# Attention values in 64x64 quarters of the array, with the next scores between their two halves

## The chip, the cores and the metric

The kernel runs on one core of one Trainium2 chip. The metric is the device time of one launch in microseconds, as the median of several runs. One launch was also profiled, and every number taken from the profile belongs to that one execution.

## The reference

Eight batches of twelve attention heads, each with 448 tokens of 64 elements. Queries and keys are normalised by their root mean square, and the outputs of the heads, put side by side, are the rows of a feed-forward block.

```python
q_n, k_n = rmsnorm(q, g_q), rmsnorm(k, g_k)          # over the 64 elements
scores = q_n @ k_n.T / sqrt(64)
attn = softmax(scores)                               # over the keys
x = (attn @ v)                                       # (8, 12, 448, 64) -> (3584, 768)
h = x @ w_in                                         # (768, 1024)
solu = h * softmax(h)
ln = (solu - mean) / sqrt(var + 1e-6) * g_ln
out = ln @ w_out                                     # (1024, 768)
```

All of it is in fp32.

## The kernel before, in words

There are three stages: attention, the product with `w_in`, and the product with `w_out`. The second and third use a Strassen-like scheme of seven products (`products`, `outer_product`), with sums of blocks made by GpSimd. This text is about the first stage and its end.

**Quads.** Attention goes through 24 quads of four heads (`for m in range(NQ)`, NQ = 24). A quad is two pairs, `a = 2*m` and `b = 2*m + 1`; a pair holds two heads. The 448 keys of a head are three chunks of 128 (`kc` = 0, 1, 2) and a last chunk of 64. The code makes these units, in an order that is written out by hand and kept as it stands on every engine:

- `scores(n, kc)`: four matrix products of 64 rows by 64 columns of the array. Row half = head, column half = half of the 128 keys. They go into one two-bank PSUM tile (tag `t`, three of them). ScalarE (ACT) then makes the exponentials `E` (line 802).
- `scores_last(m)`: the same for the last 64 keys of both pairs (line 825).
- `values_last(m)`: the values of these last keys. Four 64x64 products open the accumulation of the output `o` of each pair (line 858).
- `values(n)`: the values of the three chunks, for one pair. Six products of 128 rows by 64 columns: all 128 keys of a chunk are contracted at once, and the two heads take the two column halves (line 869).
- `sums(m)`: the denominators of the softmax, by products with ones, 128 rows by 32 columns (line 891).
- `inverse(m)` and `divide(m)`: VectorE (DVE) inverts the sums, GpSimd (POOL) copies some of them across partitions (line 910), and VectorE spreads the inverses with a transpose (line 917) and multiplies `o` by them (line 918). `divide(m)` is put behind the first unit of the next quad.
- `store_x(m)`: the quad's result goes to DRAM, on the SP queue.

In a quad TensorE (PE) gets: scores a0, a1, a2, last, b0, b1, b2, `values_last`, values a, values b, sums. Beside it, ACT squares the queries and keys of two quads ahead (`squares`, line 672), multiplies those of the next quad by the gain (`gain`, line 727), computes reciprocal roots (lines 697, 698) and takes part in the conversion of `w_in` (lines 535, 536). DVE sums squares (line 680), transposes queries and keys (line 723) and adds exponentials (line 839). POOL folds the row sums (lines 690, 691), normalises (line 713) and adds exponentials (line 848).

**PSUM.** Six of the eight banks are the three `t` tiles. The other two have tag `o`: each pair's output takes one bank as a tile of its own. In the second stage the products `B` and `D` take them.

**The end of the stage.** After quad 22 (counted from 0) `load_x(0)` brings the first 256 rows of x back from DRAM, and `sizes(0)` squares them on ACT to check their size (line 951). It stands on ACT ahead of all exponentials of quad 23. In the quads 22 and 23 VectorE makes the additions of exponentials that POOL makes elsewhere (`on_vector`).

Of the kernel before, what the change touches and what calls it, by code (L numbers as in the profile page):

```python
# [9 lines left out]
FP32 = mybir.dt.float32  # L10
# [3 lines left out]
AF = mybir.ActivationFunctionType  # L14
OP = AluOpType
# [351 lines left out]
def fast_path(  # L367
# [24 lines left out]
    nc = tc.nc  # L392
    B, H, S, D = q.shape
    DM, DFF = moe_w_in.shape
    P = 128
    NJ = S // P
    NB = S // 32
    NP = H // 2
    NQ = B * NP // 2
# [4 lines left out]
    NG = NT // 2  # L404
# [11 lines left out]
    first, middle, banks_in = ExitStack(), ExitStack(), ExitStack()  # L416
# [201 lines left out]
    st = {}  # L618
    quads = {}
# [105 lines left out]
    def gain(n):  # L725
        d = st[n]
        nc.scalar.activation(d["qkT"][:, 0], d["qkT"][:, 0], AF.Copy, scale=gcol[:, KF : KF + 1])
# [32 lines left out]
    def warm_up():  # L760

        w = work.tile([P, 2, S], FP32, tag="r", name="warm", bufs=1)[:, 0]
        nc.vector.memset(w, 0.0)
        o = ps_t.tile([P, S], FP32, tag="o", name="pt", bufs=2)
        for _ in range(5):
            nc.tensor.matmul(o, w[:, 0:P], w, start=True, stop=True)

# [5 lines left out]

    def transpose_rows(n, s):
        d = st[n]
        d["pt", s] = ps_t.tile([P, S], FP32, tag="o", name="pt", bufs=2)
        for j in range(4):
            nc.tensor.transpose(d["pt", s][:, j * R : (j + 1) * R], d["qk"][:, s, j], ident[0:R, 0:R])

# [24 lines left out]
    def scores(n, kc):  # L804
        d = st[n]
        s = ps_t.tile([P, 2, 512], FP32, tag="t", name="s")

        for c in range(0, P, D):
            for h in range(2):
                hh = slice(h * D, (h + 1) * D)  # L810
                keys = slice(NJ * c + kc, NJ * (c + D - 1) + kc + 1, NJ)
                nc.tensor.matmul(  # L812
                    s[c : c + D, h, 0:S], d["qkT"][hh, 1, keys], d["qkT"][hh, 0, :],
                    start=True, stop=True,
                )
        exponentials(d, kc, s)
# [16 lines left out]
    def on_vector(m):  # L833
        return m >= NQ - 2

    def add(n):
        d = st[n]
        d["es"] = work.tile([P, 2, S], FP32, tag="es", name="es")
        nc.vector.tensor_tensor(d["es"], d["E", 0], d["E", 1], OP.add)  # L839

    def whole(n):
        return on_vector(n // 2) or n % 2 == 0

    def add_more(n):
        d = st[n]
        if whole(n):
            e = nc.vector if on_vector(n // 2) else nc.gpsimd
            e.tensor_tensor(d["es"], d["es"], d["E", 2], OP.add)  # L848

    def values_last(m):  # L850

        d = quads[m]
        for i in range(2):
            o = st[2 * m + i]["o"] = ps_t.tile([P, S], FP32, tag="o", name="o", bufs=2)
        for h in range(2):
            for i in range(2):
                pp = slice(i * D, (i + 1) * D)
                nc.tensor.matmul(  # L858
                    st[2 * m + i]["o"][h * D : (h + 1) * D, :], d["vl"][pp, h], d["E", NJ][pp, h],
                    start=True, stop=False,  # L860
                )

    def values(n):


        d = st[n]
        for kc in range(NJ):
            for h in range(2):
                nc.tensor.matmul(  # L869
                    d["o"][h * D : (h + 1) * D, :], quads[n // 2]["v"][:, n % 2 + 2 * h, kc], d["E", kc][:, h],  # L870
                    start=False, stop=(kc == NJ - 1),
                )
# [37 lines left out]
                nc.gpsimd.tensor_copy(rc[o : o + 32, :, t], rc[a : a + 32, :, t])  # L910

    def divide(m):
        xo = quads[m]["xo"] = work.tile([P, 2, S], FP32, tag="xo", name="xo", bufs=1)
        for i in range(2):
            n = 2 * m + i
            r = work.tile([P, NB, 32], FP32, tag="r", name="r", bufs=1)
            nc.vector.transpose(r, quads[m]["rc"][:, i].rearrange("p t b -> p (t b) ()").to_broadcast([P, NB, 32]))
            nc.vector.tensor_tensor(xo[:, i], st[n]["o"], r.rearrange("d b i -> d (b i)"), OP.mult)
            del st[n]

    def store_x(m):
        b, hp = divmod(2 * m, NP)
        xo = quads.pop(m)["xo"]
        rows = xd[b].rearrange("(g h i d) t -> h d g i t", h=2, i=2, d=D)
        for h in range(2):
            nc.sync.dma_start(rows[h][:, hp // 2], xo[h * D : (h + 1) * D])
# [5 lines left out]
    banks = []  # L932
# [12 lines left out]
    def sizes(g):  # L945

        x = gs[g, "x"].rearrange("p c t -> p (c t)")
        n = HD * 2 * P
        sm = gs[g, "s"] = xs.tile([P, 3, HD, P], FP32, tag="x", name="xsum")
        for i in range(2):  # L950
            nc.scalar.activation(
                sm.rearrange("p k c t -> p (k c t)")[:, 0:n], x[:, i * n : (i + 1) * n], AF.Square,
                accum_out=xmax[:, 2 * g + i : 2 * g + i + 1],
            )

# [20 lines left out]
    def products(g, done):  # L976


        k = {}
        n = DFF // 2  # L980

        def mul(bank, a, i, begin=True):
            a11, a12, a21, a22 = gs[g, "A"]
            sm = gs[g, "s"]
            a = {"a11": a11, "a12": a12, "s3": a21, "a22": a22, "s1": sm[:, 0], "s2": sm[:, 1], "s4": sm[:, 2]}[a]
            if begin:
                tag = "t" if bank in "AC" or bank == "B" and g == NG - 1 else "o"
                k[bank] = ps_t.tile([P, 512], FP32, tag=tag, name=bank, bufs=3 if tag == "t" else 2)[:, 0:n]
            for c in range(HD):
                nc.tensor.matmul(  # L990
                    k[bank], a[:, c], w_in[i][:, c],
                    start=begin and c == 0, stop=c == HD - 1, skip_group_check=not begin,
                )

        def part(name, bank):
            k[name] = sums_in.tile([P, 512], FP32, tag="part", name=name, bufs=4)[:, 0:n]
            nc.scalar.copy(k[name], k[bank])

        def plus(row, col, bank, x):
            t = 2 * g + row
            d = mt.setdefault(t, {})
            out = half_of(t, col)
            top = small.tile([P, 1], FP32, tag="top", name="top")
            nc.vector.tensor_tensor_reduce(
                out, k[bank], k[x], 1.0, d.get("top", -3.4e38), OP.add, OP.max, top
            )
            d["top"] = top

        def p1():
            mul("A", "a11", 0)
            part("q1", "A")

        def p2():
            mul("C", "a12", 1)
            plus(0, 0, "C", "q1")

        def p6():
            mul("A", "s2", 5, False)  # L1020
            part("u2", "A")

        def p5():
            mul("B", "s1", 3)

        def p7():
            mul("A", "s3", 4, False)
            part("u3", "A")
            plus(1, 1, "B", "u3")

        def p4():
            mul("D", "a22", 6)
            plus(1, 0, "D", "u3")
            done(1)

        def p3():
            mul("B", "s4", 2, False)
            plus(0, 1, "B", "u2")
            done(0)

        return {1: p1, 2: p2, 3: p3, 4: p4, 5: p5, 6: p6, 7: p7}
# [275 lines left out]
    def unit(f, steps=4):  # L1317
        nonlocal now
        f()
        now += steps  # L1320
        due = [x for x in todo if x[0] <= now]
        todo[:] = [x for x in todo if x[0] > now]
        for _, g in sorted(due, key=lambda x: x[0]):
            g()
# [26 lines left out]
    def step(m):  # L1351
        if m in sets:
            sets[m].pop(0)()
# [11 lines left out]
    with tc.manual_schedule():  # L1365
# [19 lines left out]
        for m in range(NQ):  # L1385
            a, b = 2 * m, 2 * m + 1

            def outputs():
                values_last(m)
                values(a)  # L1390


            next1 = m + 1 < NQ
# [52 lines left out]
                load_v(m + 1)  # L1446
            if m == 1:
                load(m + 3)
            unit(lambda: scores(a, 0))
            if m == 1:  # L1450
                gain(3)
            store_x(m - 1)
            if early:
                qk_transpose(a + 2)
                if next3 and m > 1:
                    load(m + 3)
            unit(lambda: scores(a, 1))
            unit(lambda: scores(a, 2))
            unit(lambda: scores_last(m))
            unit(lambda: scores(b, 0))  # L1460
# [4 lines left out]
            if not on_vector(m):  # L1465
                add_more(a)
            unit(lambda: scores(b, 2))
            if next2:
                squares(a + 4)
                squares(b + 4)  # L1470
                row_sums(a + 4)
            if next1:
                gain(a + 2)
                gain(b + 2)
            if next2:
                row_sums(b + 4)
                fold_sums(m + 2)
# [1 line left out]
            if on_vector(m):  # L1479
                add_more(a)  # L1480
                add_more(b)
            unit(outputs)
            step(m - 2)
            begin(m)
            step(m - 1)
# [4 lines left out]
                load_next()  # L1490
            if m == 3:
                norm_gain()
            unit(lambda: values(b))
            if m == NQ - 1:
                block_sums(0, 0)
                block_sums(0, 1)
# [4 lines left out]
                later(1, lambda m=m: divide(m))  # L1501
            if m == NQ - 2:
                load_x(0)
                sizes(0)
        divide(NQ - 1)
        store_x(NQ - 1)
        first.close()
# [185 lines left out]
```

## Time and profile before

| | |
|---|---|
| median of 3 runs | 802.65 us (802.65 to 802.79) |
| the profiled execution, its own time | 803.36 us |
| its span, first to last instruction | 801.6 us |
| TensorE clock granted | 0.999 |
| busy: PE, DVE, ACT, POOL | 98%, 77%, 59%, 65% |
| attention stage | from the start to about 316 us |
| one quad of it in the steady part | 12.51 us |

Busy time is the time in which at least one instruction of an engine is recorded as running. For PE it says little on speed, because up to four small products run side by side: a busy share of 98% may hide a rate that is lower than it could be. Each fp32 matrix product is recorded as two instructions, so a unit of four products appears as x8. The chain of waits goes back from the last instruction to what released it, and so shows which engine's time adds up to the span.

### The profile page before, as it was taken

The numbers are of one execution on the slowest core, as the hardware profiler recorded it, in microseconds if no ns is written. First come the engines' busy times: TensorE is split into PE (matmuls) and PEld (weight loads), VectorE is DVE, ScalarE is ACT, GpSimd is POOL, SyncE is SP. The second block draws the span as 40 slices with busy tenths as digits, with TensorE's granted clock in tenths as the row PEclk, the third lists the DMA queues.
The fourth block names the chain that finished last, engine by engine and source line by source line (L and its number), as shares of the span: only waits on it lengthen the run. The fifth ranks groups of instructions, "written<-read, shape, count | busy, mean of one in ns | idle before, by whom it ended". The sixth has DMA issues, their size and how long they took to land.

```text
span 801.6 us, 14271 instructions
## 1 busy us (share of the span) xinstructions
PE 788.1 (98%) x4854; PEld 462.7 (58%) x4854; DVE 613.7 (77%) x1202; ACT 472.2 (59%) x783; POOL 523.1 (65%) x664
## 2 busy tenths in 40 slices
PE   8999999999999999999999999999999999999997
PEld 4344444444444443444444444444789999999996
DVE  6787989989888896488878666777896776866945
ACT  6677878878778774376766544444515455464420
POOL 2666777778876784234456467668698777877861
PEclk9999999999999999999999999999999999999999
DMA  9878889897787832445554435552757457366312
GB/s 169 164 174 156 175 194 186 194 189 161 169 157 169 158 102 75 136 117 155 152 146 131 113 98 141 142 137 52 190 167 233 147 183 264 123 221 223 112 61 83
DMA packets 269598, 122.68 MB, mean 153 GB/s; under 512 B 187596, under 2 KB 254668, under 8 KB 269516
## 3 DMA queue, kind: packets, MB, share of 16 engines
q1 hardware_dynamic: 254332, 111.78, 55.9%
q10 hardware_dynamic: 15184, 9.90, 4.5%
q8 instruction: 40, 0.66, 0.3%
q14 instruction: 42, 0.34, 0.1%
HBM read 84.94 MB, written 36.70 MB: 152 GB/s over the span
## 4 chain that ended last, share of the span: by engine, by line
PE 87%; DVE 3%; DMA 2%; SPq 2%; POOL 2%; ACT 2%; issue 1%; DVEq 0%; ACTq 0%; POOLq 0%
PE A L1205 14%; PE A L990 13%; PE o L869 12%; PE s L812 12%; PE B L990 8%; PE B L1205 7%; PE C L990 4%; PE sm L891 4%; PE D L990 4%; PE C L1205 3%; PE s L825 2%; PE o L858 2%; SPq L636 1%; DMA xg<-xd 1%; ACT E L802 1%
## 5 line engine op out<-in xcount | busy, mean ns | idle before, releaser
L802 ACT ACTIVATE E<-s 128x896 f32<-128x896 f32 x168 | 138.8, 937 | 8.3 <-PE s L812 7.8
L812 PE MATMUL s<-qkT 64*64 64x448 f32 x1152 | 120.1, 545 | 1.0 <-ACT qkT L786 0.6
L869 PE MATMUL o<-E,v 128*64 128x448 f32 x576 | 113.8, 543 | 0.0
L1079 POOL TENSOR_TENSOR he<-he,mhalf 128x1 f32<-128x1 f32 x28 | 27.4, 977 | 102.5 <-DVE he L1078 97.4
L812 PEld LDWEIGHTS s<-qkT 64*64 64x64 f32 x1152 | 48.0, 163 | 59.4 <-ACT E L802 29.3
L1205 PE MATMUL A<-w_out,sums 128*128 128x192 f32 x392 | 79.9, 327 | 1.6 <-POOL sums L1185 1.2
L869 PEld LDWEIGHTS o<-E,v 128*64 128x64 f32 x576 | 39.1, 137 | 72.2 <-issue 68.0
L1205 PE MATMUL B<-w_out,sums 128*128 128x192 f32 x392 | 79.8, 326 | 0.5 <-DVE P L1267 0.5
L713 POOL TENSOR_TENSOR qkn<-qk,ny 128x896 f32<-128x896 f32 x46 | 77.2, 1699 | 3.8 <-DMA qk<-in_q_dram 1.5
L848 POOL TENSOR_TENSOR es<-es,E 128x896 f32<-128x896 f32 x22 | 46.4, 2110 | 48.8 <-ACT sq L672 34.0
L990 PE MATMUL B<-w_in,xsum 128*128 128x512 f32 x168 | 76.7, 592 | 0.0
L990 PE MATMUL A<-w_in,xg 128*128 128x512 f32 x168 | 74.6, 593 | 0.0
L1061 ACT ACTIVATE u<-h,hmax 128x1024 f32<-128x1024 f32 x28 | 32.2, 1148 | 66.8 <-DVE hmax L1055 66.8
L1205 PEld LDWEIGHTS A<-w_out,sums 128*128 128x128 f32 x392 | 66.1, 190 | 2.4 <-POOL sums L1185 1.5
L1205 PEld LDWEIGHTS B<-w_out,sums 128*128 128x128 f32 x392 | 66.2, 190 | 0.8 <-DVE P L1267 0.8
L839 DVE TENSOR_TENSOR es<-E 128x896 f32<-128x896 f32 x48 | 53.9, 1124 | 2.7 <-ACT E L802 2.7
L990 PEld LDWEIGHTS B<-w_in,xsum 128*128 128x128 f32 x168 | 31.9, 190 | 40.2 <-issue 39.2
L990 PEld LDWEIGHTS A<-w_in,xg 128*128 128x128 f32 x168 | 31.8, 190 | 40.1 <-issue 39.3
L690 POOL COPY ss<-part 32x56 f32<-32x56 f32 x92 | 47.0, 511 | 5.9 <-DVE part L680 1.4
L680 DVE TENSOR_REDUCE part<-sq 128x28 f32<-128x896 f32 x46 | 47.9, 1080 | 3.9 <-ACT sq L672 1.6
L723 DVE STREAM_TRANSPOSE qkT<-qkn 128x896 f32<-128x896 f32 x46 | 48.4, 1087 | 0.0
L563 POOL TENSOR_TENSOR w_out<-w_out 128x384 f32<-128x384 f32 x44 | 45.0, 1028 | 1.3
(153 smaller groups left out, 1651.0 us busy)
## 6 DMA issues: line engine op xcount, KB each, us to landing
ur<-ud SPq DMA_DIRECT2D x60, 256.0 KB, 4.6
ud<-ub SPq DMA_DIRECT2D x112, 128.0 KB, 2.3
xd<-xo SPq DMA_DIRECT2D x48, 224.0 KB, 3.0
qk<-in_q_dram SPq DMA_DIRECT2D x92, 112.0 KB, 3.1
qk<-in_k_dram SPq DMA_DIRECT2D x92, 112.0 KB, 3.0
v<-in_v_dram SPq DMA_DIRECT2D x24, 384.0 KB, 4.3
out_dram<-P SPq DMA_DIRECT2D x19, 384.0 KB, 4.2
raw<-in_moe_w_in_dram SPq DMA_DIRECT2D x12, 512.0 KB, 5.3
```

Source lines behind the costliest of these rows:

```text
L563: nc.gpsimd.tensor_tensor(o, p, q, OP.subtract)
L680: nc.vector.tensor_reduce(norms[m]["part"][:, i], st[n]["sq"], AX, OP.add)
L690: e.tensor_copy(ss[g * 32 : g * 32 + 32], part[o * 32 : o * 32 + 32])
L713: e.tensor_tensor(d["qkn"].rearrange("p (s b) d -> p s b d", s=2), d["qk"].rearrange("p s (b d) -> p s b d", d=32), y.rearrange("p (s b) - ...
L723: nc.vector.transpose(d["qkT"].rearrange("p s t -> p (s t)"), d["qkn"].rearrange("p b d -> p (b d)"))
L802: nc.scalar.activation(d["E", kc], s[:, :, 0:S], AF.Exp)
L812: nc.tensor.matmul(s[c : c + D, h, 0:S], d["qkT"][hh, 1, keys], d["qkT"][hh, 0, :], start=True, stop=True,)
L839: nc.vector.tensor_tensor(d["es"], d["E", 0], d["E", 1], OP.add)
L848: e.tensor_tensor(d["es"], d["es"], d["E", 2], OP.add)
L869: nc.tensor.matmul(d["o"][h * D : (h + 1) * D, :], quads[n // 2]["v"][:, n % 2 + 2 * h, kc], d["E", kc][:, h], start=False, stop=(kc == NJ ...
L990: nc.tensor.matmul(k[bank], a[:, c], w_in[i][:, c], start=begin and c == 0, stop=c == HD - 1, skip_group_check=not begin,)
L1205: nc.tensor.matmul(k[bank], a[:, c].rearrange("p a i -> p (a i)"), w_out[:, area, i, c], start=begin and c == 0, stop=c == KC - 1, skip_gr ...
```

## The change

**Quarters.** For the quads 1 to 22 (`halved(m)`) the values of both pairs are made by 64x64 products (`values_part`). A chunk's 128 keys are split in two halves of 64 rows. In part 0 pair a uses the keys in rows 0 to 63 and pair b those in rows 64 to 127, and in part 1 they exchange. So in each part a pair's bank is written from one row half only. Each part has 12 products instead of the 6 of `values(n)`.

**The first scores between.** Ahead of part 1 each row half must be done with the bank that the other row half is to write. `turn(m)` puts an empty instruction on ACT that waits for part 0's last product, and part 1's first product waits for it. Between the parts PE gets `scores(a + 2, 0)`, the first scores of the next quad, which are therefore missing at that quad's head. The quads 0 and 23 keep `values(a)`, `values(b)`.

**One tile.** Both pairs' outputs are one two-bank tile; `divide` makes one transpose and one product of 896 columns instead of two of 448 each. The tiles of the start (`pt`) and `B`, `D` of the second stage are paired likewise.

**Order on ACT.** `gain(a + 2)` goes ahead of the squares and `gain(b + 2)` behind the turn. `sizes(0)` goes behind the last exponentials of quad 23, and writes its squares into a work tile.

**One addition** of the last pair (47) goes from DVE to POOL.

The SP queue has the same instructions in the same order.

```diff
     def transpose_rows(n, s):
         d = st[n]
-        d["pt", s] = ps_t.tile([P, S], FP32, tag="o", name="pt", bufs=2)
+        if s == 0:
+            d["pt"] = ps_t.tile([P, 2, 512], FP32, tag="o", name="pt", bufs=1)
+        d["pt", s] = d["pt"][:, s, 0:S]
...
     def add_more(n):
         d = st[n]
         if whole(n):
-            e = nc.vector if on_vector(n // 2) else nc.gpsimd
+            e = nc.vector if on_vector(n // 2) and n < 2 * NQ - 1 else nc.gpsimd
...
     def values_last(m):
         d = quads[m]
+        o = d["o"] = ps_t.tile([P, 2, 512], FP32, tag="o", name="o", bufs=1)
         for i in range(2):
-            o = st[2 * m + i]["o"] = ps_t.tile([P, S], FP32, tag="o", name="o", bufs=2)
+            st[2 * m + i]["o"] = o[:, i, 0:S]
...
+    def values_part(m, part):
+        first = None
+        for kc in range(NJ):
+            for i in range(2):
+                d = st[2 * m + i]
+                pp = slice((part ^ i) * D, (part ^ i) * D + D)
+                for h in range(2):
+                    x = nc.tensor.matmul(
+                        d["o"][h * D : (h + 1) * D, :], quads[m]["v"][pp, i + 2 * h, kc], d["E", kc][pp, h],
+                        start=False, stop=(part == 1 and kc == NJ - 1),
+                    )
+                    first = first or x
+        if part == 0:
+            quads[m]["half"] = x
+        else:
+            behind(first, quads[m]["turn"])
...
+    def turn(m):
+        x = quads[m]["turn"] = nc.scalar.nop()
+        behind(x, quads[m]["half"])
...
     def divide(m):
-        for i in range(2):
-            r = work.tile([P, NB, 32], FP32, tag="r", name="r", bufs=1)
-            nc.vector.transpose(r, quads[m]["rc"][:, i].rearrange("p t b -> p (t b) ()").to_broadcast([P, NB, 32]))
-            nc.vector.tensor_tensor(xo[:, i], st[n]["o"], r.rearrange("d b i -> d (b i)"), OP.mult)
+        r = work.tile([P, 2 * NB, 32], FP32, tag="r", name="r", bufs=1)
+        nc.vector.transpose(r, d["rc"].rearrange("p i t b -> p (i t b) ()").to_broadcast([P, 2 * NB, 32]))
+        nc.vector.tensor_tensor(xo, d["o"][:, :, 0:S], r.rearrange("d (i b) x -> d i (b x)", i=2), OP.mult)
...
             def outputs():
                 values_last(m)
-                values(a)
+                if halved(m):
+                    values_part(m, 0)
+                else:
+                    values(a)
...
-            unit(lambda: scores(a, 0))
             if m == 1:
+                unit(lambda: scores(a, 0))
                 gain(3)
+            else:
+                unit(lambda: scores(a, 1))
...
             unit(lambda: scores(b, 2))
+            if not next1:
+                sizes(0)
+            if next1:
+                gain(a + 2)
             if next2:
                 squares(a + 4)
                 squares(b + 4)
                 row_sums(a + 4)
-            if next1:
-                gain(a + 2)
-                gain(b + 2)
...
             unit(outputs)
+            if halved(m):
+                turn(m)
+                gain(b + 2)
...
-            unit(lambda: values(b))
+            if halved(m):
+                unit(lambda: scores(a + 2, 0))
+                unit(lambda: values_part(m, 1))
+            else:
+                unit(lambda: values(b))
...
             if m == NQ - 2:
                 load_x(0)
-                sizes(0)
```

More of the change, by code (lines that the diff above doesn't have):

```diff
@@ L763, in warm_up @@
         nc.vector.memset(w, 0.0)
-        o = ps_t.tile([P, S], FP32, tag="o", name="pt", bufs=2)
+        o = ps_t.tile([P, 2, 512], FP32, tag="o", name="pt", bufs=1)[:, 0, 0:S]
         for _ in range(5):
@@ L839, in add, with halved @@
         nc.vector.tensor_tensor(d["es"], d["E", 0], d["E", 1], OP.add)
+    def halved(m):
+        return 0 < m < NQ - 1
     def whole(n):
@@ L861, in values_last, with behind @@
                 )
+    def values_part(m, part):
[14 more added lines that the diff above has]
+            behind(first, quads[m]["turn"])
+    def behind(x, y):
+        tc.add_manual_dep(
+            getattr(x, "ins", x), getattr(y, "ins", y).name,
+            mybir.DependencyInfo(mybir.DependencyClass.Sync, mybir.DependencyReason.DATA),
+            reason="row tiles change banks",
+        )
+    def turn(m):
+        x = quads[m]["turn"] = nc.scalar.nop()
+        behind(x, quads[m]["half"])
     def values(n):
@@ L912, in divide @@
     def divide(m):
-        xo = quads[m]["xo"] = work.tile([P, 2, S], FP32, tag="xo", name="xo", bufs=1)
-        for i in range(2):
-            n = 2 * m + i
-            r = work.tile([P, NB, 32], FP32, tag="r", name="r", bufs=1)
-            nc.vector.transpose(r, quads[m]["rc"][:, i].rearrange("p t b -> p (t b) ()").to_broadcast([P, NB, 32]))
-            nc.vector.tensor_tensor(xo[:, i], st[n]["o"], r.rearrange("d b i -> d (b i)"), OP.mult)
-            del st[n]
+        d = quads[m]
+        xo = d["xo"] = work.tile([P, 2, S], FP32, tag="xo", name="xo", bufs=1)
+        r = work.tile([P, 2 * NB, 32], FP32, tag="r", name="r", bufs=1)
+        nc.vector.transpose(r, d["rc"].rearrange("p i t b -> p (i t b) ()").to_broadcast([P, 2 * NB, 32]))
+        nc.vector.tensor_tensor(xo, d["o"][:, :, 0:S], r.rearrange("d (i b) x -> d i (b x)", i=2), OP.mult)
+        for i in range(2):
+            del st[2 * m + i]
     def store_x(m):
@@ L949, in sizes @@
         sm = gs[g, "s"] = xs.tile([P, 3, HD, P], FP32, tag="x", name="xsum")
+        y = sm.rearrange("p k c t -> p (k c t)")
+        if g == 0:
+            y = work.tile([P, 2 * NB, 32], FP32, tag="sq", name="sq", bufs=2).rearrange("p b d -> p (b d)")
         for i in range(2):
             nc.scalar.activation(
-                sm.rearrange("p k c t -> p (k c t)")[:, 0:n], x[:, i * n : (i + 1) * n], AF.Square,
+                y[:, 0:n], x[:, i * n : (i + 1) * n], AF.Square,
                 accum_out=xmax[:, 2 * g + i : 2 * g + i + 1],
@@ L986, in mul @@
             if begin:
-                tag = "t" if bank in "AC" or bank == "B" and g == NG - 1 else "o"
-                k[bank] = ps_t.tile([P, 512], FP32, tag=tag, name=bank, bufs=3 if tag == "t" else 2)[:, 0:n]
+                if bank in "AC" or bank == "B" and g == NG - 1:
+                    k[bank] = ps_t.tile([P, 512], FP32, tag="t", name=bank, bufs=3)[:, 0:n]
+                else:
+                    if "BD" not in k:
+                        k["BD"] = ps_t.tile([P, 2, 512], FP32, tag="o", name="BD", bufs=1)
+                    k[bank] = k["BD"][:, "BD".index(bank), 0:n]
             for c in range(HD):
@@ L1456, in fast_path @@
                     load(m + 3)
-            unit(lambda: scores(a, 1))
+            if m == 1:
+                unit(lambda: scores(a, 1))
             unit(lambda: scores(a, 2))
@@ L1492, in fast_path @@
                 norm_gain()
-            unit(lambda: values(b))
+            if halved(m):
+                unit(lambda: scores(a + 2, 0))
+                unit(lambda: values_part(m, 1))
+            else:
+                unit(lambda: values(b))
             if m == NQ - 1:
```

## The prediction

> **What bounds the kernel now.** I read the page first: busy times and the chain that ended last.
>
> ```profile
> PE 788.1 (98%) x4854; PEld 462.7 (58%) x4854; DVE 613.7 (77%) x1202; ACT 472.2 (59%) x783; POOL 523.1 (65%) x664
> ...
> PE 87%; DVE 3%; DMA 2%; SPq 2%; POOL 2%; ACT 2%; issue 1%; DVEq 0%; ACTq 0%; POOLq 0%
> ```
>
> PE is busy for 98% and holds 87% of the chain, so time comes only from what PE executes, from gaps in it, or from the rate at which small products run side by side. For the rate I read the chain over a steady stretch (start, duration, what).
>
> ```profile
> 205.31 0.75 PE s L825 x8
> 206.06 2.25 PE s L812 x24
> 208.32 0.75 PE o L858 x8
> 209.07 4.66 PE o L869 x24
> 213.73 1.65 PE sm L891 x32
> 215.38 2.45 PE s L812 x24
> ```
>
> The reader is to see that no engine but PE is in it, and the rates. 64x64 products: 0.75 us for 8 instructions, 2.25 for 24, so 0.094 each. 128x64 products: two beside each other instead of four, so 24 should take 24 x 0.188 = 4.51; the line has 4.66, which is 0.15 more. The trace's single records show where: 64x64 products start in groups of four every 0.376 us, values in groups of two every 0.376, but from the last group of line 858 to the first of line 869 it is 0.485, and to the next 0.427. That is 0.11 + 0.05 = 0.16 us for going from 64x64 to 128x64. The groups of sums (0.189 apart) and of scores show the same at their heads: 2.45 against 2.25 is 0.20, and 1.65 against 32 x 0.047 = 1.50 is 0.15. Quad 3 confirms it: a 128-row transpose between its two values costs each of them the entry (2.40 and 2.41 instead of 2.25). So a quad of 12.51 us pays three changes of shape, half a microsecond together.
>
> The gaps of PE are few: of those after the start, the longest but one is in quad 23. In order of time on PE, then ACT (start, duration; in brackets the idle time before and what ended it):
>
> ```profile
> 302.68 2.52 PE L812 MATMUL s<-qkT 64*64 64x448 f32 x24
> 306.21 0.98 PE L825 MATMUL s<-qkT 64*64 64x448 f32 x8 [1.01 <-ACT E L802]
> 307.02 2.62 PE L812 MATMUL s<-qkT 64*64 64x448 f32 x24
> 309.47 0.93 PE L858 MATMUL o<-E,vl 64*64 64x448 f32 x8
> ```
> ```profile
> 303.45 0.84 ACT L951 ACTIVATE xsum<-xg 128x768 f32<-128x768 f32 x1 [5.08 <-DMA xg<-xd]
> 305.26 5.74 ACT L802 ACTIVATE E<-s 128x896 f32<-128x896 f32 x7
> ```
>
> ACT waits 5.08 us for the DMA of x with the size check at its head; the seven exponentials stand behind it, all three `t` tiles fill up and PE stops. In other quads line 825 starts 2.34 us after the first scores, here 3.53; later pieces are 0.06 and 0.19 late. Together 1.44 us.
>
> **What the Trainium skill says.** TensorEngine Tiling (Array Packing), Key Properties: changing the tiling mode, not just the tile, drains TensorE. The trace agrees and prices it at 0.15 to 0.20 us. The same page, Gotcha 1: different row tiles can't use one PSUM bank at the same time; that is why the turn must exist. The trace has no case of it, but `values_last` already writes each bank from one row half, at the full 0.376 us per group of four. PSUM — Partial Sum Buffer, Engine vs sequencer instructions: a sequencer instruction waits for earlier ones to be dispatched, not to complete. The trace agrees: ACT's semaphore events for the squares stand at 220.91 to 221.15, while the exponential ahead of the last one was still running (to 221.36). No price of a page is used.
>
> **The change part by part.**
>
> *Quarters.* Removed: 12 products (24 instructions) of 128x64. Added: 24 products (48 instructions) of 64x64, at 0.094 each 4.51 us, the same as 24 x 0.188. The order of the quarters differs from that of the scores (row halves change every second product), but these four are also all different, and line 858 shows four quarters with four separate streams at full rate. What goes is the entry of 0.16 us, since everything from the first scores to part 1 is now 64x64. The entry to sums (0.15) stays, from 64x64 instead of 128x64: not seen before, so it may be anything from 0 (a gain of another 0.15 per quad) to 0.30 (the saving is lost there); I take 0.15, as all the entries seen lie at 0.15 to 0.20. The scores moved between the parts keep the shape, and the next quad's a1 pays the 0.20 that a0 paid. 22 quads x 0.16 = **3.5 us less**.
>
> *The turn.* Part 1's first product waits for ACT, which waits for part 0's last product. Behind it on PE are the rest of part 1, the sums and the next quad. With zero at the first scores after the sums, PE's new course is: a1 to b2 and `values_last` until 5.34, part 0 until 7.59, next a0 until 8.34, part 1 until 10.60. Part 0's last product ends at 7.77 (a record is 0.54 long). PE's end at 220.835 and ACT's next event at 220.908 give a hop of 0.07; two hops make 7.95, a weight load 0.14, so 8.1 against 8.34: 0.25 us to spare. ACT must have reached the turn by then. Its six exponentials start at 1.08 (after the reciprocal roots, as now), 0.80 apart, and end at 6.0; gain to 6.6; squares to 8.3. If ACT's sequencer is one instruction ahead, it is at the turn by 7.5. So I take 0. From both sides: no gain, since the wait only adds; at worst the turn falls behind the finished squares, 8.3 + 0.07 + 0.14 = 8.5, and 0.2 us per quad. Behind it on ACT stand `gain(b + 2)` (due 5 us later), the conversion and the next a0's exponential, whose tile is wanted again only by the next a2.
>
> *Scores ahead.* a0 of the next quad is wanted at 7.59, its gain done at 6.6, its queries transposed on DVE at about 5.2. E takes an eighth buffer of eight; the ninth is written only after part 1 has read the first. ACT's tightest point was b2, whose tile came free at 219.74 and which began at 219.90, 0.17 us later; six exponentials instead of seven leave 0.24. Nothing is late, 0.
>
> *One divide.* DVE saves two starts: 2 x (0.65 + 0.63) = 2.56 becomes about 2.1 (a transpose of 896 columns takes 1.09 on line 723). It lies beside PE, and brings the transposes forward until they meet POOL's normalise (ends at 220.68, the transpose of it began at 220.87), some 0.15. The quad gets shorter by about the same, so POOL's fold, which releases ACT's roots just in time (215.70, roots done at 216.36, scores ready at 216.31), stays where it was relative to PE. One tile for both banks must be read out before `values_last`, 3 us later: 0. In the second stage B's release is the last of its group either way: 0.
>
> *Size check.* The 1.44 us of quad 23 go: x lands at about 300 and ACT comes to it at about 305, after its exponentials. Its reader on POOL is wanted 5 us after the end of the sums. **1.4 us less.** The last addition on POOL takes 2.1 us where DVE took 1.0; it is wanted 2 us later by the sums, and the block sums behind it are still 5 us early: 0.
>
> Sum: 3.5 + 1.4 = 4.9. The profiled execution took 803.36 us (span 801.6, 1.8 around it), 0.7 above the median: 798.5, and from the median of 802.65, **797.7 us**.
>
> **Rivals.**
> 1. *Only the check counts.* The change of shape is not saved but paid at the sums or the parts (0.16 per quad). For: the sums change rows and columns at once. Against: each entry in the trace costs 0.15 to 0.20 whatever the pair of shapes. 802.65 - 1.4 = 801.2, no change.
> 2. *The turn holds PE* (slower). If ACT reaches the turn only once both squares have completed, and each hop takes 0.2 instead of 0.07, part 1 starts at 8.8 instead of 8.34: 0.45 per quad. 22 x (0.45 - 0.16) = 6.4, less 1.4: 807.6. It decides from a stall of 0.22 us per quad (0.16 + 1.4 / 22). For: the spare time is only 0.25 us. Against: the events of ACT run ahead of its engine.
> 3. *The sums' entry goes too*, in part: 22 x 0.1 less, 795.5.
>
> **How the numbers follow.** Main course 0.70, rival 1 or a small stall of the turn 0.13, rival 2 with its milder forms 0.10, rival 3 0.07. The measurement can tell about 0.2% (1.6 us) from no change. Faster: main, rival 3 and a part of rival 1, 0.81; same 0.09; slower 0.10. The range goes from rival 3, 795.5, to the worst that I worked out for the turn, 0.2 per quad: 22 x (0.2 - 0.16) = 0.9, less 1.4, 802.1. It takes in rival 1; the worse part of rival 2 and a full loss of the sums' entry stay out.
>
> **What would show it.** Right: between the sums no engine but PE in the chain, a quad of 12.35 us, line 858's successor at 2.25 per part, quad 23 without a gap before line 825's successor. Wrong: idle time before part 1 released by ACT's sequencer, parts slower than 2.25, or sums above 1.65.

## The result and the profile after

The changed kernel takes 802.2 us (median of 20 runs, 801.27 to 803.93); the kernel before took 803.43 us in the same comparison (20 runs, 802.49 to 804.52). The ratio is 0.9985, 95% interval 0.9979 to 0.9991: 1.2 us less, where the prediction had 4.9 less. The profiled execution has a span of 800.4 us instead of 801.6.

First the page of the changed kernel: busy times, and shares of the chain that ended last.

```profile
PE 786.5 (98%) x5382; PEld 468.7 (59%) x5382; DVE 609.0 (76%) x1153; ACT 473.1 (59%) x783; POOL 524.3 (66%) x665
...
PE 86%; DVE 5%; SPq 2%; issue 2%; ACT 1%; DMA 1%; POOL 1%; DVEq 0%; ACTq 0%; POOLq 0%
```

PE has lost 1.6 us of busy time and still holds the chain: the bound is the same. The chain of waits over a steady stretch (start, duration, what):

```profile
205.88 2.25 PE s L814 x24
208.14 0.75 PE o L864 x8
208.89 2.25 PE o L878 x24
211.15 0.75 PE s L814 x8
211.90 2.25 PE o L878 x24
214.15 1.65 PE sm L927 x32
215.80 1.70 PE s L814 x16
```

This is what the prediction asked for. Each part has 2.25 for 24 instructions, so two parts take 4.50 where the two values took 4.66; the next quad's scores lie between them; the sums still pay their entry (1.65); no other engine is in it. A steady quad, from the start of its sums to that of the next, is 12.37 us instead of 12.52 (given as 12.51 above).

Quad 23, on PE and then on ACT, in order of time:

```profile
302.17 1.77 PE L814 MATMUL s<-qkT 64*64 64x448 f32 x16
303.76 0.93 PE L827 MATMUL s<-qkT 64*64 64x448 f32 x8
304.51 2.44 PE L814 MATMUL s<-qkT 64*64 64x448 f32 x24
306.76 0.93 PE L864 MATMUL o<-E,vl 64*64 64x448 f32 x8
```
```profile
303.25 4.97 ACT L804 ACTIVATE E<-s 128x896 f32<-128x896 f32 x6 [3.80 <-PE s L814]
308.05 0.90 ACT L990 ACTIVATE sq<-xg 128x768 f32<-128x768 f32 x1
```

No gap is left on PE, and the check of `x` (line 990) stands behind the exponentials. So every step that the prediction named in the attention stage is there, and the time isn't. The table takes the span apart by the starts of PE's instructions. It also has a second profile of each kernel, taken later (experiments 10 and 11).

| us | before | before, 2nd | after | after, 2nd |
|---|---|---|---|---|
| start to the sums of quad 0 | 23.39 | 23.43 | **25.26** | **25.25** |
| to the sums of quad 1 | 14.72 | 14.69 | 15.26 | 15.24 |
| to the sums of quad 22 | 263.18 | 263.18 | 260.13 | 260.14 |
| to the sums of quad 23 | 13.71 | **12.97** | 11.64 | 11.62 |
| to the second stage | 1.27 | 1.27 | 1.27 | 1.27 |
| second stage, first to last product | 252.03 | 252.02 | **252.89** | **252.88** |
| third stage, first to last product | **227.23** | 227.90 | 227.80 | 227.82 |

The three rows between the sums of quad 0 and of quad 23 hold what was predicted: 291.6 - 287.0 = 4.6 us less (3.8 against the second profile of before). Two costs stand against it. The start is 1.85 us later, and the second stage is 0.86 longer. The start of the changed kernel on PE, and of the kernel before:

```profile
8.74 1.16 PE L780 MATMUL pt<-ident,x 112*128 112x112 f32 x8 [0.47 <-PE pg L491]
11.11 2.52 PE L814 MATMUL s<-qkT 64*64 64x448 f32 x24 [1.21 <-ACT qkT L788]
13.56 0.60 PE L780 MATMUL pt<-ident,x 112*128 112x112 f32 x4
15.30 0.60 PE L780 MATMUL pt<-ident,x 112*128 112x112 f32 x4 [1.14 <-ACT qkT L786]
```
```profile
10.58 2.52 PE L812 MATMUL s<-qkT 64*64 64x448 f32 x24 [0.62 <-ACT qkT L786]
13.03 0.98 PE L778 MATMUL pt<-ident,x 112*128 112x112 f32 x8
```

Two things are to be seen. The first scores begin at 11.11 instead of 10.58. And the second pair's eight transposes, one group at 13.03 before, are cut into four at 13.56 and four at 15.30, with a wait for ACT's line 786 between. ACT of the changed kernel shows the other side:

```profile
10.00 0.64 ACT L786 ACTIVATE qkT<-pt,gcol 128x448 f32<-128x448 f32 x1 [0.47 <-PE pt L780]
...
14.60 0.65 ACT L786 ACTIVATE qkT<-pt,gcol 128x448 f32<-128x448 f32 x1
```

The first copy out of `pt` needs only the first four transposes, but it waits for all eight. The later one stands behind three exponentials (from 12.19 on), and the next transposes, which write the other bank, wait for it. Both banks are one tile since the change; the explanation to be tested is that each wait here is for the whole tile (experiments 1 to 4).

The second stage shows the same, on PE and on DVE:

```profile
365.44 1.98 PE L1033 MATMUL BD<-w_in,xg 128*128 128x512 f32 x4
```
```profile
364.69 0.69 DVE L1049 CUSTOM_DVE_ANT_0 h<-BD,u 128x512 f32<-128x512 f32 x1 [2.02 <-ACT u L1040]
365.31 0.08 DVE L1049 DVE_READ_ACCUMULATOR2_ANT top<- 128x1 f32 x1
```

From the last `A` product's start to the first `BD` product's it is 0.28 us longer than the usual 0.43: that product, bank D's first, starts at 365.44, when DVE has finished reading bank B (its event stands at 365.40). The next start is 0.10 late as well, and the pair comes once more at 419.

### The profile page after: what moved, and what is told of

Read it like the earlier page. It is cut to its first block, busy times and chain, and to the rows that moved or that the text cites. A ratio compares the mean times of both kernels' runs of the same rounds, so it can differ in the third digit from the quotient of the medians.

```text
span 800.4 us, 15291 instructions
## 1 busy us (share of the span) xinstructions
PE 786.5 (98%) x5382; PEld 468.7 (59%) x5382; DVE 609.0 (76%) x1153; ACT 473.1 (59%) x783; POOL 524.3 (66%) x665
## 4 chain that ended last, share of the span: by engine, by line
PE 86%; DVE 5%; SPq 2%; issue 2%; ACT 1%; DMA 1%; POOL 1%; DVEq 0%; ACTq 0%; POOLq 0%
PE A L1248 14%; PE s L814 13%; PE o L878 12%; PE BD L1033 11%; PE A L1033 11%; PE B L1248 7%; PE sm L927 5%; PE C L1033 5%; PE C L1248 3%; PE s L827 2%; PE o L864 2%; SPq L636 1%; DVE ub L1137 1%; DVE bs L1116 1%; PE o L905 1%
## 5 line engine op out<-in xcount | busy, mean ns | idle before, releaser
L804 ACT ACTIVATE E<-s 128x896 f32<-128x896 f32 x168 | 141.4, 932 | 12.8 <-PE s L814 11.6
L814 PE MATMUL s<-qkT 64*64 64x448 f32 x1152 | 123.9, 544 | 1.6 <-ACT qkT L788 1.2
L878 PE MATMUL o<-E,v 64*64 64x448 f32 x1056 | 107.1, 536 | 0.0
L853 POOL TENSOR_TENSOR es<-es,E 128x896 f32<-128x896 f32 x23 | 49.1, 2137 | 51.4 <-DVE es L841 51.4
L878 PEld LDWEIGHTS o<-E,v 64*64 64x64 f32 x1056 | 40.2, 133 | 58.4 <-issue 58.4
L1033 PE MATMUL BD<-w_in,xsum 128*128 128x512 f32 x156 | 71.2, 592 | 0.0
L841 DVE TENSOR_TENSOR es<-E 128x896 f32<-128x896 f32 x48 | 57.1, 1193 | 0.7 <-ACT E L804 0.7
L723 DVE STREAM_TRANSPOSE qkT<-qkn 128x896 f32<-128x896 f32 x46 | 50.9, 1106 | 4.1 <-POOL qkn L713 4.1
L1033 PEld LDWEIGHTS BD<-w_in,xsum 128*128 128x128 f32 x156 | 29.5, 190 | 37.5 <-issue 35.1
L1248 PE MATMUL A<-w_out,s 128*128 128x192 f32 x224 | 45.6, 326 | 0.5 <-ACT u L1260 0.5
```

The lines of the kernel that those rows point to most:

```text
L723: nc.vector.transpose(d["qkT"].rearrange("p s t -> p (s t)"), d["qkn"].rearrange("p b d -> p (b d)"))
L804: nc.scalar.activation(d["E", kc], s[:, :, 0:S], AF.Exp)
L814: nc.tensor.matmul(s[c : c + D, h, 0:S], d["qkT"][hh, 1, keys], d["qkT"][hh, 0, :], start=True, stop=True,)
L878: x = nc.tensor.matmul(d["o"][h * D : (h + 1) * D, :], quads[m]["v"][pp, i + 2 * h, kc], d["E", kc][pp, h], start=False, stop=(part == 1 a ...
L1033: nc.tensor.matmul(k[bank], a[:, c], w_in[i][:, c], start=begin and c == 0, stop=c == HD - 1, skip_group_check=not begin,)
L1248: nc.tensor.matmul(k[bank], a[:, c].rearrange("p a i -> p (a i)"), w_out[:, area, i, c], start=begin and c == 0, stop=c == KC - 1, skip_gr ...
```

## Experiments

The lines of kernels 1, 2, 3, 8 and 9 stand some lines further down than those of the changed kernel, because of a helper at the top.

### 1. The start in tiles of its own

```diff
-        o = ps_t.tile([P, 2, 512], FP32, tag="o", name="pt", bufs=1)[:, 0, 0:S]
+        o = two[1].tile([P, S], FP32, tag="o", name="pt", bufs=2)
...
-        if s == 0:
-            d["pt"] = ps_t.tile([P, 2, 512], FP32, tag="o", name="pt", bufs=1)
-        d["pt", s] = d["pt"][:, s, 0:S]
+        d["pt", s] = two[1].tile([P, S], FP32, tag="o", name="pt", bufs=2)
```

`two` is a pool for these two banks alone, closed and opened again behind the start; the rest is the changed kernel.

> The changed kernel, but the start's transposes (pt) again go into two one-bank tiles of their own, so that the two-bank tile of the values comes after them; all else as in the changed kernel. Theory (a whole tile is what waits are made for: the first copy on ACT waits for all eight transposes instead of four, and the second four transposes wait for ACT's copy of the first): the first scores start at 10.6 instead of 11.1 us, the idle 1.14 us before the last transposes goes, the sums of quad 0 start at 23.4 instead of 25.3, and the time falls by 1.8 us against the changed kernel, to about 0.9963 of the kernel before. Rival (0.53 of it is a slower warm-up of TensorE in that one execution, not the tiles): 1.3 us less, and the first scores at 11.1 in this profile too.

Measured: 800.32 us, ratio to before 0.9961 (0.9947 to 0.9974). PE at the start:

```profile
10.63 2.52 PE L820 MATMUL s<-qkT 64*64 64x448 f32 x24 [0.62 <-ACT qkT L794]
13.07 0.98 PE L786 MATMUL pt<-ident,x 112*128 112x112 f32 x8
```

The wait of 1.21 is 0.62 again and the eight transposes are one group. The sums of quad 0 begin at 23.43, and the second stage at 311.88 instead of 313.56. Both pieces of the start's delay come from the paired tile. Of the 1.8 us gained by the sums of quad 0, 1.7 are left at the second stage: quad 1 waits 0.50 us for ACT at its head instead of 0.34.

### 2. B and D in tiles of their own

The pool `two` is here opened again ahead of the second stage; the start's tiles stay paired.

```diff
-                    if "BD" not in k:
-                        k["BD"] = ps_t.tile([P, 2, 512], FP32, tag="o", name="BD", bufs=1)
-                    k[bank] = k["BD"][:, "BD".index(bank), 0:n]
+                    k[bank] = two[1].tile([P, 512], FP32, tag="o", name=bank, bufs=2)[:, 0:n]
```

> The changed kernel, but B and D of the second stage are again one-bank tiles of their own. Theory (a whole tile is what waits are made for: D's first product waits for DVE's read of B, which in two of the groups is late): the two gaps before the first D product, 0.38 and 0.46 us, go; the second stage takes 252.03 us from its first to its last product instead of 252.89, and the time falls by 0.9 us against the changed kernel, to about 0.9974 of the kernel before. Rival (the gaps come from DVE's work falling otherwise against TensorE's, since the stage starts 2.7 us earlier): the gaps stay and the ratio stays at 0.9985.

Measured: 800.76 us, 0.9976 (0.9962 to 0.999). The second stage is 252.02 long and its gaps are gone; the start is as late as in the changed kernel (first scores at 11.04).

### 3. Both

> The changed kernel with both of these: start tiles and B, D in one-bank tiles of their own; the pairs' outputs still in one two-bank tile. Theory: 1.8 + 0.9 = 2.7 us less than the changed kernel, so about 3.9 us less than the kernel before, ratio 0.9951; if the 0.57 us that the third stage lost also comes back, 0.9944. Rival (the loss is in the phase of the engines and not in the tiles): 0.9985.

Measured: 799.66 us, 0.995 (0.9936 to 0.9963). The second stage starts at 311.89 and is 252.03 long, with quads of 12.37: the two costs are separate and add up, except for 0.2 us that quad 1 loses again (it takes 15.48 instead of 15.26). This version, 3.6 us below before, beats both kernels; only the outputs of a quad are still one tile.

### 4. The tiles alone

The kernel before with all three pairings and the merged divide, and nothing else of the change.

> The kernel before with nothing but the tiles paired: pt at the start, the two outputs of a quad with one divide, and B with D. No quarters, size check where it was. Theory: the start is 1.8 us later and the second stage up to 0.9 us longer, so 1.8 to 2.7 us slower than before, ratio 1.0022 to 1.0034. Rival (the pairing costs nothing by itself, the losses come with the quarters): 1.0000.

Measured: 805.29 us, 1.0028 (1.0018 to 1.0038): slower by itself. PE at the start shows the same wait of 1.14 us for line 786, the second stage is 252.88 long. A steady quad stays at 12.52.

### 5. The quarters alone

The kernel before with quarters, turn, scores between and the order of the gains; outputs in two tiles, two divides, the size check where it was.

```diff
-            unit(lambda: values(b))
+            if halved(m):
+                unit(lambda: scores(a + 2, 0))
+                unit(lambda: values_part(m, 1))
```

> The kernel before with the quarters alone: parts, turn, the next quad's first scores between them, and the order of the gains. Every output and every B, D keeps a one-bank tile of its own, two divides per quad, size check ahead of quad 23's exponentials. Theory (one change of shape less per quad, the turn costs nothing): a quad of 12.37 us instead of 12.52, 3.0 to 3.3 us less than before; the size check still holds up quad 23 by about 1.4. Ratio 0.9960. Rival (the merged divide is needed to keep ACT and POOL on time): quads of over 12.4 us with idle time of TensorE released by ACT.

Measured: 802.79 us, 0.9996 (0.9987 to 1.0004). This was a miss. A steady quad is 12.49, not 12.37. PE in a steady quad of this kernel, and the same of the changed kernel:

```profile
220.59 1.06 PE L861 MATMUL o<-E,vl 64*64 64x448 f32 x8
221.34 2.56 PE L875 MATMUL o<-E,v 64*64 64x448 f32 x24
...
224.34 2.56 PE L875 MATMUL o<-E,v 64*64 64x448 f32 x24
226.83 0.96 PE L924 MATMUL sm<-E,ones 128*32 128x224 f32 x16
```
```profile
220.33 0.93 PE L864 MATMUL o<-E,vl 64*64 64x448 f32 x8
221.08 2.43 PE L878 MATMUL o<-E,v 64*64 64x448 f32 x24
...
224.09 2.44 PE L878 MATMUL o<-E,v 64*64 64x448 f32 x24
226.45 0.96 PE L927 MATMUL sm<-E,ones 128*32 128x224 f32 x16
```

From line 861 to 875 it is 0.75 in both, but every piece lasts 0.12 to 0.13 longer, and from part 1 to the sums it is 2.49 instead of 2.36. The single records say why: in a group one quarter starts on time (221.337) and the other three 0.13 later (221.468 to 221.481), and so it stays until the sums wait for all of them. What made the three late is on DVE, here the second divide of this kernel and then the one divide of the changed kernel:

```profile
219.99 0.62 DVE L951 TENSOR_TENSOR xo<-o,r 128x448 f32<-128x448 f32 x1
```
```profile
218.88 1.09 DVE L953 TENSOR_TENSOR xo<-o,r 128x896 f32<-128x896 f32 x1
```

The second divide ends at 220.61. Of `values_last`, one quarter's first record starts at 220.585 and the other three's at 220.665 to 220.679, just behind it. The first product writes pair a's bank, which the first divide has left; the second writes pair b's and waits, and the other two start behind it. The merged divide ends at 219.97, 0.36 us ahead of `values_last` at 220.33. In quad 2 the second divide ends at 45.36, 0.39 behind the start of `values_last` at 44.98, and the quad takes 12.85 instead of 12.45. Quad 23 of this kernel lost more as well: its size check got `x` at 304.58, and PE stood idle for 1.65 us. The Trainium skill (TensorEngine Tiling (Array Packing), Key Properties) says that tiles operate independently. This trace agrees: one quarter runs 0.13 us ahead of the other three. It also shows the other face of it: the delay isn't absorbed, it stays until the next change of shape.

### 6. The size check alone

```diff
                 load_x(0)
-                sizes(0)
...
             unit(lambda: scores(b, 2))
+            if not next1:
+                sizes(0)
```

The squares of the check also go into a work tile, as in the changed kernel.

> The kernel before with nothing but the size check of the first rows moved behind quad 23's exponentials and into a work tile. Theory: quad 23's gap of about 1.4 us goes and nothing else changes, so 1.4 us less, ratio 0.9982. Rival (the wait is only put off, to the block sums that follow the check): 1.0000.

Measured: 802.11 us, 0.999 (0.9983 to 0.9997): 0.6 us less between the medians, 0.2 to 1.4 by the interval. From the sums of quad 22 to those of quad 23 it is 12.25, against 13.71 in the first profile of before and 12.97 in the second. (In this profile quad 1, which the edit doesn't touch, is 0.40 us longer than in the first profile of before, with a wait of 0.80 for ACT at its head instead of 0.40.) The step is right; what it is worth depends on when `x` lands.

### 7. Quarters and size check, without pairs

> The kernel before with quarters and size check and no paired tile anywhere, two divides per quad, the last addition on DVE. Theory (the pairing and the merged divide bring nothing in any place): 4.4 us less than before, as the changed kernel with all its start and second-stage tiles apart, ratio 0.9945 to 0.995. Rival (the merged divide is worth something): at least 0.5 us slower than that, and quads longer than 12.37 us.

The last addition of pair 47 stays on DVE here. Measured: 801.46 us, 0.9982 (0.9974 to 0.9989). The quads take 12.48, as in 5, so the theory that the merged divide is worth nothing falls; against kernel 3 the second stage starts 2.75 us later.

### 8. No scores between the parts

Kernel 3 with the next quad's first scores behind part 1.

```diff
-                unit(lambda: scores(a + 2, 0))
                 unit(lambda: values_part(m, 1))
+                unit(lambda: scores(a + 2, 0))
```

> The changed kernel with start tiles and B, D apart, but the next quad's first scores stand behind part 1 instead of between the parts, so that nothing covers the turn. Theory (part 0's last product is done 0.16 us after the next group could start, two hops of 0.07 and a weight load of 0.14): a gap of 0.4 to 0.5 us before part 1 in each of 22 quads, 9 to 11 us more than with the scores between, ratio about 1.007. Rival (ACT comes late to the turn, or a hop is dearer): a gap of 0.8 us or more, ratio above 1.016; then the scores covered the turn with nothing to spare.

Measured: 806.96 us, 1.0047 (1.0032 to 1.0062), a quad of 12.73: 0.36 more. PE's weight loads behind part 0 show the wait (in brackets the idle time before and what ended it):

```profile
201.46 0.21 PEld L884 LDWEIGHTS o<-E,v 64*64 64x64 f32 x8 [0.91 <-ACTq L902]
```

Part 0's last record ends at 201.325, ACT's event stands at 201.391, and part 1's first product starts at 201.459: 0.07 there and 0.07 back. Its start is 0.69 after that of part 0's last group (200.770), where groups follow each other every 0.376, and the next group is 0.05 late: 0.31 + 0.05 are the 0.36. That is less than the 0.4 to 0.5 expected, and the second stage starts 7.24 us later than in kernel 3 instead of 9 to 11. In the changed kernel ACT's event is at 211.213, so that part 1's first product, at 211.719 behind the scores, could start some 0.44 earlier by the same hop of 0.07 (an estimate). So the turn needs its cover, and has it with room to spare.

### 9. Two divides on the one tile

Kernel 3 with the division cut in two again.

```diff
-        r = work.tile([P, 2 * NB, 32], FP32, tag="r", name="r", bufs=1)
-        nc.vector.transpose(r, d["rc"].rearrange("p i t b -> p (i t b) ()").to_broadcast([P, 2 * NB, 32]))
-        nc.vector.tensor_tensor(xo, d["o"][:, :, 0:S], r.rearrange("d (i b) x -> d i (b x)", i=2), OP.mult)
+        for i in range(2):
+            r = work.tile([P, NB, 32], FP32, tag="r", name="r", bufs=1)
+            nc.vector.transpose(r, d["rc"][:, i].rearrange("p t b -> p (t b) ()").to_broadcast([P, NB, 32]))
+            nc.vector.tensor_tensor(xo[:, i], d["o"][:, i, 0:S], r.rearrange("d b i -> d (b i)"), OP.mult)
```

> The best version (start and B/D in tiles of their own, both outputs of a quad in one tile) with the division cut in two again: per half a transpose of 448 and a multiply of 448, as in the kernel before. Main theory: the margin is the division's, not the tile's: two halves end 0.5 to 0.6 us later than one whole, after the next quad's values_last want to begin, so each steady quad grows from 12.37 to about 12.49 as in e5 (one or more quarters lag 0.1 to 0.2 us until the sums): 20 quads x 0.12 = 2.4 us, stage 2 starts at about 314.3 instead of 311.9, ratio about 0.998. Since both halves now wait for the last multiply, it could be a little more than in e5 (up to 0.2 per quad). Rival: the tile alone did it; then quads stay at 12.37 and the ratio at 0.995.

Measured: 802.09 us, 0.9988 (0.9981 to 0.9995), a quad of 12.49, the second stage from 314.69. The chain over a steady stretch shows `values_last` at 0.88 instead of 0.75:

```profile
220.78 0.88 PE o L870 x8
```

Here all quarters wait for the last divide, and again 0.12 per quad is lost. So two divides lose it, whether the outputs are one tile or two.

### 10 and 11. A second profile of both kernels

> The changed kernel, a second profile. Asked: is the third stage's length (227.80 us in the first profile, 227.23 in the kernel before) a property of the kernel or of the execution? If of the kernel: 227.8 again within 0.1. If of the execution: anything from 226.4 to 227.7 as in the other runs. The first stage should end at 313.5 to 313.7 and the second be 252.9 long again.

> The kernel before, a second profile. If the third stage's length is a property of the kernel, 227.2 again within 0.1; otherwise anything from 226.4 to 227.8. The second stage should begin at 316.2 to 316.7 and be 252.0 long again.

The changed kernel repeats its stages within 0.04 us. The kernel before does not: the third stage takes 227.90 instead of 227.23, and quad 23 is 0.74 shorter. PE and ACT in quad 23 of this second profile:

```profile
305.50 0.98 PE L825 MATMUL s<-qkT 64*64 64x448 f32 x8 [0.29 <-ACT E L802]
```
```profile
302.74 0.84 ACT L951 ACTIVATE xsum<-xg 128x768 f32<-128x768 f32 x1 [4.35 <-DMA xg<-xd]
```

The load of `x` was issued at the same time (296.35 against 296.34), but ACT could begin at 302.74 instead of 303.45, and PE's stall at line 825 is 0.29 instead of 1.01. In the third stage of this profile PE waits 1.00 us for ACT's copy of `u` (at 579.64), which stands behind a copy of `ur`, which waits for a transfer; the first profile has no such wait there (`ur` is loaded back from DRAM; `u`, and `q` below, are copied out of PSUM):

```profile
579.12 0.62 ACT L1160 COPY a<-ur 128x512 f32<-128x512 f32 x1 [2.17 <-DMA ur<-ud]
```
```profile
580.00 0.92 PE L1205 MATMUL A<-w_out,s 128*128 128x192 f32 x4 [1.00 <-ACT u L1217]
```

Over the profiles of all kernels the third stage took 226.4 to 227.9, and that of the kernel before alone 227.23 and 227.90. So the 0.6 by which the first two profiles differ there can't be put down to the change.

One wait in this stage does go with the kernel. Some 2.7 us into it, PE of the changed kernel stands until ACT has copied `q`, for 0.57 us in the first profile and 0.56 in the second:

```profile
569.56 0.89 PE L1248 MATMUL A<-w_out,sums 128*128 128x192 f32 x4 [0.57 <-ACT q L1260]
```

Neither profile of before has it. The kernels 1, 2, 3, 7, 8 and 9, which have both the quarters and the moved check, have it too (0.25 to 0.56 us); 4, 5 and 6, which lack one or both, don't. Whether it makes the stage longer is not shown, because waits further on change from one execution to the next, as in before.

## Why the prediction was wrong

| term | predicted | found |
|---|---|---|
| quarters, 22 quads | -3.5 | -3.25 |
| size check | -1.4 | -1.3 or -0.6 |
| one tile at the start (`pt`) | not in the sum | +1.85 |
| one tile for B and D | 0 | +0.86 |
| third stage | 0 | +0.6 or -0.1, by execution |
| sum | -4.9 | -1.2 |

"Found" compares the first profile of after with the first of before, and with the second where two numbers stand. The quarters are the rows to the sums of quad 1 and of quad 22: 3.05 less in the second; in the first 0.54 more, but with 0.75 of moved scores in it, so 0.21 less, of which 0.06 is a shorter wait for ACT at its head (0.34 instead of 0.40). The size check is the row of quad 23 with the 0.75 that left it put back. Of the 3.7 us that are missing, the two costs of tiles are 2.7; the rest lies in the size check or in the third stage, by execution, and 0.25 in the quarters.

**The step that failed** is "One tile", at the end of *One divide*. The prediction gave it one sentence on the outputs and one on B: "In the second stage B's release is the last of its group either way: 0". It asked when the tile is released, not who else now waits for it. Whichever of the two is released last, D's first product now waits for DVE's read of B, which costs 0.38 us at 365 and 0.46 at 419. The `pt` tiles of the start, in the front of the diff, were not costed at all. Experiments 1, 2 and 3 take the two costs away one by one and together and get the time back: 799.66 us against 802.2, 2.5 of the 2.7 us of the two terms. The rivals had the wait in the wrong place. Rival 2 expected it at the turn, and rival 1's number, 801.2, came near the result for a reason that isn't there: the change of shape is saved (12.37).

**Right.** The saving per steady quad was 0.151 against 0.16, the sums kept their entry of 1.65, and rival 3 fell. Of the missing 0.25, 0.17 is this 0.009 in 19 steady quads; the quads 2 and 3 saved only 0.07 and 0.10. In quad 2 even the merged divide comes too late: it ends at 46.74, and `values_last` starts behind it at 46.79. The turn was costed at 0, and the two hops at 0.07 each; experiment 8 shows both, and the spare time was some 0.44 instead of 0.25. The prediction's sum has 7.95 where 7.77 and two hops of 0.07 make 7.91, and it adds a weight load of 0.14; in experiment 8 the load starts at 201.457, beside its product, and adds nothing to the hop. ACT's event for the turn (211.213) came while the second squares were running (to 211.641), as the prediction had it with the Trainium skill (PSUM — Partial Sum Buffer, Engine vs sequencer instructions): such an instruction doesn't wait for earlier ones to complete.

**Right by luck.** "One tile for both banks must be read out before `values_last`, 3 us later: 0" has the right value and a wrong margin. In the kernel before the second divide ends at 207.40 and `values_last` starts at 208.14: 0.74 us, not 3.

```profile
206.78 0.62 DVE L918 TENSOR_TENSOR xo<-o,r 128x448 f32<-128x448 f32 x1
```
```profile
208.14 0.93 PE L858 MATMUL o<-E,vl 64*64 64x448 f32 x8
```

The unit a0, which leaves the quad's head, is 0.75 us of what lay between. With two divides nothing would have been left; the merged one ends 0.36 us ahead. "One divide" was costed at 0 as something that lies beside PE; it carries 0.12 us per quad, 2.4 us over 20 quads, and 0.4 in quad 2 (experiments 5, 7, 9). By itself it is worth nothing to the quad: in experiment 4 it ends 1.14 us ahead of `values_last`, and the quad stays at 12.52. The margin of 0.74 could have been read from the trace of before.

**Mis-sized.** The size check's 1.44 us was one execution's stall. By the second profile it is 0.6 to 0.7, and experiment 6 gives 0.6 between medians. A stall that ends with a DMA's landing should have had a range of its own.

**Open.** What makes the transfers of `x` and `ur` land earlier or later, `x` by 0.7 us, was not tried. What makes ACT's copy of `q` late in the third stage of the changed kernel was not looked into. Whether merging the outputs' tile has a worth of its own, beside allowing one divide, shows only in experiments 7 and 9, whose starts of the second stage hardly differ (314.65 and 314.69).

## What to carry to other kernels

When two buffers become one tile, list every reader and writer of either half and ask which of them will now wait for each other: here one late reader held a writer that never touched its bank. Pair them only where one instruction really takes both, as the divide does here, and give the other uses of the same memory tiles of their own. And when work is moved out of the head of a loop, everything that had to be finished by a later point of it comes nearer to that point by as much.

## What was not expected of the hardware

- Products in the four 64x64 quarters ran as separate streams. Quarters that started 0.13 us late stayed late through some 6 us of products, and this was paid once, at the next change of shape (experiment 5).
- Handing a bank from one row half to the other through another engine's event took 0.14 us from record end to next start, and cost 0.36 us of PE's pace where nothing lay between (experiment 8).
- The same program's load of `x`, issued at the same time in two executions, landed 0.7 us apart, and moved a stall of PE by as much (experiment 11).
